# Attention and a routed expert layer on one core: the product of a head pair moved behind the next pair's first two scores, the sums of v kept in its tile, the gate arithmetic moved to GpSimd

## The chip, the cores and the metric

The kernel runs on one core of one Trainium2 chip. The metric is the device time of one execution in microseconds: 448.46 us, the median of two runs (448.41 and 448.5). The profile is of one further execution with a span of 449.2 us. A slot below is a unit of the written order, not of time.

## What is computed

Two layers follow one another. The first is attention over 8 batches and 12 heads, 448 positions of 64, with a softmax whose denominator has an extra 1:

```python
scores = scale * np.matmul(q, k.transpose(0, 1, 3, 2))
m = np.max(scores, axis=-1, keepdims=True)
e = np.exp(scores - m)
attn = e / (np.sum(e, axis=-1, keepdims=True) + np.exp(-m) + 1e-09)
return np.matmul(attn, v)
```

Multiplied through by exp(m), the weights are exp(s) / (sum of exp(s) + 1). The second layer takes the 3584 rows of 768 numbers, finds the nearest of 8 expert vectors by cosine and applies that expert:

```python
logits = xn @ en.T / tau
expert_idx = np.argmax(logits, axis=1)
gate_w = probs[np.arange(N), expert_idx]     # softmax of the logits, at the chosen expert
h = np.maximum(x[mask] @ w1[e], 0.0)         # 768 x 1024
out[mask] = gate_w[mask, None] * (h @ w2[e]) # 1024 x 768
```

## The kernel before

**Tiling.** Work on attention goes by head pairs: 12 heads make 6 pairs in a batch (`NP`), 48 pairs in all. A pair's queries and keys are transposed by TensorE with an identity (`front_qk`, L193 and L194), so that each of the two heads holds 64 partitions, and copied to SBUF: keys by ScalarE (L203), queries by VectorE (L208). The scores come with the key position in the partitions. Tiles 0, 1 and 2 hold 128 key positions of both heads (L235); tile 3 holds the last 64 positions of the two heads, one head in each half of the partitions (L241). ScalarE takes the exponential (L246, L248), VectorE subtracts one (L254, L257). What is multiplied with v is exp(s) - 1, and the sum over v itself is added afterwards: hence "sums of v".

**The product** (`attend`, L270 and L275) has one accumulation for each head. Its weights are `vab`: 64 columns of v and 64 columns of ones, so that 64 output rows hold the product and 64 the sum of exp(s) - 1. In the kernel before, both heads have the order v, ones; the product is always in rows 0 to 63. ScalarE turns the sums into 1/(1 + sum/449) by Ln (L285) and Exp of the negative (L289), VectorE adds the sum of v and multiplies (`normalise`, L303), and a bf16 copy for the experts follows (`low`, L312). A square of x for the norm follows (`square`: GpSimd for the first pairs, ScalarE from pair 11 on).

**Sums of v.** GpSimd adds the four pieces of v (`sum_v`, L180 to L182). A matmul with a column of ones adds over the partitions (L198), two pairs at a time, into two free columns of the tile of the transposes. VectorE copies them to SBUF as `sv` (L213), where `normalise` reads them as scalars.

**Router.** When a batch's six pairs are done, `router_mm` multiplies with the expert vectors and with ones (L335, 24 matmuls), the result is copied (L341) and transposed (`router_tok`, L349). VectorE finds the chosen expert of each token (`router_logits`), a matmul counts them (`router_pick`, L414), VectorE finds the most frequent expert (`router_count`), and GpSimd loads its index and fetches its weights by seven DMAs (`fetch`, L447). The gate is worked out by `router_pow` (a square root as a power on GpSimd, L375), `router_exp` (VectorE, L381 to L383), `router_act` (ScalarE, L389) and `router_gate` (VectorE, L395 to L408). Tokens of other experts have a path of their own at the end.

**Experts.** A batch has 15 chunks: eight of h (6 matmuls each, L487) and seven of y (8 or 16 matmuls, L515, L534). A chunk fills one PSUM tile `work`, which VectorE or ScalarE then empties (L495, L497, L505, L507). The chunks of a batch are strewn over six later pairs, twelve pairs behind its attention (`LAG`).

**Order.** The order on every engine is written out by hand. `put(slot, fn)` files a piece under a number; the pieces are emitted in rising order of it, and each engine runs its own in that order. Pair g has the numbers from 8g (`NSLOT` = 8). A piece's number says where it stands in the queues, and not when it runs. Chunks stand at the offsets `FILL`: three in an even slot and two in an odd one. `late` has, for each offset, the number at which the chunk's tile is emptied, and whether VectorE does it. Before, the product of pair g stands at 3.35 of the slot after its own, ahead of score tile 3 of the next pair (its neighbours are score tile 2 at 3.3 and tile 3 at 3.4).

**Buffers in PSUM.** `work` has 2 tiles of one bank (chunks, score tile 3, warm-up, the router's transposes), `big` 2 tiles of two banks (transposes, score tiles 0 to 2, the router product), `av` one tile of two banks (the product). A new tile waits until the last but one of its kind is emptied, for `av` the last one.

Of the kernel before, what the change touches and what calls it, by code (L numbers as in the profile page):

```python
# [28 lines left out]
FILL = ((0.8, 3.2, 5.6), (0.8, 5.6))  # L29
# [7 lines left out]
def build_consts(k):  # L37
# [26 lines left out]
    for s in range(2):  # L64
        va = pool.tile([128, 4, 4, 64], F32R, name=f"vab{s}")
        for h in range(2):
            nc.vector.tensor_copy(
                out=va[:, :, 2 * h + 1, :],
                in_=k.ones_f[:, 0:1].unsqueeze(2).broadcast_to([128, 4, 64]),
            )  # L70
        k.vab.append(va)


def build_late_consts(k):
# [11 lines left out]
    nc.vector.memset(k.half[:], 0.5)  # L86
    k.rr = pool.tile([128, 512], F32, name="rr")
# [98 lines left out]
def front_qk(k, g, s):  # L186
# [8 lines left out]
    if i == GP - 1:  # L195
        vs = k.va.pop(n)
        for j in range(GP):
            nc.tensor.matmul(ps[:, 0, S + j : S + j + 1], lhsT=vs[:, 2 * j : 2 * j + 2, :], rhs=k.ones_f[:],  # L198
                             start=True, stop=True)

# [5 lines left out]
    def q_out():  # L206
        qt = k.qt.tile([128, S], F32R, name="qt", tag="qt")
        nc.vector.tensor_copy(out=qt[:], in_=ps[:, 0, 0:S])  # L208
        k.qts[g] = qt
        if i == GP - 1:  # L210
            k.sv[n] = k.svp.tile([64, GP, 2], F32, name="sv", tag="sv")
            for h in range(2):
                nc.vector.tensor_copy(out=k.sv[n][:, :, h], in_=ps[64 * h : 64 * h + 64, 0, S : S + GP])  # L213

    k.put(s + 0.6, k_out)
    k.put(s + 0.7, q_out)


# [44 lines left out]
def attend(k, g, s, b=None):  # L263
# [4 lines left out]
    for h in range(2):  # L268
        r = slice(64 * h, 64 * h + 64)
        nc.tensor.matmul(  # L270
            ps[:, h, 0:S], lhsT=va[r, 3, 2 * h : 2 * h + 2, :], rhs=k.ems[g, 3][r, :], start=True, stop=False,
        )
    for j in range(3):
        for h in range(2):
            nc.tensor.matmul(  # L275
                ps[:, h, 0:S], lhsT=va[:, j, 2 * h : 2 * h + 2, :], rhs=k.ems[g, j][:, h, :],
# [3 lines left out]
    if b is not None:  # L280
        router_pick(k, b, ps[:, 0, S : S + 4 * E])

    def log():
        k.rd[g] = k.rdp.tile([128, 2, S], F32, name="rd", tag="rd")
        nc.scalar.activation(k.rd[g][64:128], ps[64:128, :, 0:S], ACT.Ln, bias=1.0, scale=1.0 / (S + 1.0))  # L285

    def recip():
        rd = k.rd.pop(g)
        nc.scalar.activation(rd[64:128], rd[64:128], ACT.Exp, scale=-1.0)  # L289
        k.avs[g] = ps, rd  # L290

    k.put(s + 1.45, log)
    k.put(s + 1.65, recip)


def normalise(k, g, s):
# [4 lines left out]
    sv = k.sv[g // GP]  # L301
    for h in range(2):
        nc.vector.scalar_tensor_tensor(  # L303
            out=x[64 * h : 64 * h + 64, :], in0=ps[0:64, h, 0:S], scalar=sv[:, g % GP, h : h + 1],
            in1=rd[64:128, h, :], op0=ALU.add, op1=ALU.mult,
# [8 lines left out]
    k.put(s + 1.6, low)  # L314
# [12 lines left out]
def router_mm(k, b, s):  # L327
# [13 lines left out]
    k.put(s + 1.75, lambda: nc.scalar.copy(out=k.rr[:, 0:S], in_=ps[:, 0:S]))  # L341


def router_tok(k, b, s):

    nc, p = k.nc, k.rp
    tp = k.work.tile([128, 4, 128], F32, name="work", tag="work")
    for t in range(4):
        nc.tensor.transpose(tp[:, t, :], k.rr[:, 128 * t : 128 * t + 128], k.ident[:])  # L349
    k.put(s + 0.8, lambda: router_logits(k, b, tp))  # L350
# [27 lines left out]
def router_exp(k, b):  # L378
    nc, p = k.nc, k.rp
    l, nrm = k.lg[b]  # L380
    nc.vector.tensor_scalar_add(nrm[:], nrm[:], 1e-6 * (S + 1.0))  # L381
    nc.vector.reciprocal(out=nrm[:], in_=nrm[:])
    nc.vector.tensor_tensor(out=l[:], in0=l[:], in1=nrm[:].unsqueeze(2).broadcast_to([128, 4, E]), op=ALU.mult)  # L383
# [8 lines left out]
def router_gate(k, b):  # L392
    nc, p = k.nc, k.rp
    gate = p.tile([128, 4], F32, name="gate", tag="gate")
    nc.vector.reduce_sum(out=gate[:], in_=k.lg.pop(b)[:], axis=AX.X)  # L395
    nc.vector.tensor_scalar_add(gate[:], gate[:], 1e-9)
    nc.vector.reciprocal(out=gate[:], in_=gate[:])
# [386 lines left out]
```

The softmax here doesn't subtract the row's maximum and nothing guards it: scores larger than these inputs give would overflow.

## Time and profile before

| what | us |
|---|---|
| time, median of two runs | 448.46 |
| span of the profiled execution | 449.2 |
| product of pair 0, 11, 46, 47 begins | 22.05, 103.36, 390.32, 396.78 |
| one exponential of 128x896 (L246, mean) | 0.915 |
| one subtraction of 128x896 (L254, mean; median) | 0.731; 0.622 |
| one half of normalise (L303, mean) | 0.677 |
| one power on GpSimd (L375, mean) | 1.160 |

A name such as L246 is a line of the kernel. PE is TensorE, PEld its loading of weights, DVE VectorE, ACT ScalarE, POOL GpSimd and SP the engine that issues most DMAs. In lists of waits a line says who waited, for whom, the sum in us, how often, and the longest. In the chain of waits a line has the start, the length and the work; it is followed back from the end of the execution, at each step to what released it. Busy time of PE is not PE at its peak, since its matmuls overlap and their ends are modelled.

### The profile page before, as it was taken

To read this page: it belongs to the slowest core of one execution; us is meant where nothing else is said; L and a number is where in the kernel's file an instruction comes from. 1 tells how busy PE (TensorE), PEld (TensorE's weight loads), DVE (VectorE), ACT (ScalarE), POOL (GpSimd) and SP (SyncE) were. 2 spreads that over 40 slices of the span, in tenths; PEclk is the share of its full clock that TensorE was granted. 3 is DMA by queue.
4 is the path that set the end of the run, shared out by engine and by line. 5 is a ranking of instruction groups with operands and counts; after the bars stand their busy time and mean duration, and the time that the engine had idled before them with its cause. 6 is when DMAs were issued, how large, how long until landed. Compare 5 with 4: busy or idle time off the path is not lost.

```text
span 449.2 us, 7412 instructions
## 1 busy us (share of the span) xinstructions
PE 402.3 (90%) x2430; PEld 239.4 (53%) x2430; DVE 338.4 (75%) x771; ACT 318.9 (71%) x440; POOL 135.6 (30%) x170
## 2 busy tenths in 40 slices
PE   7977789778989999899989999899989998999696
PEld 3545454545556556555565555665666556545243
DVE  2569987998699769996799769986999769754222
ACT  1578877787797888788787878788879878751111
POOL 4115442745156004700074003800372006105100
PEclk9699999999999999999999999999999999999889
DMA  8775345799479966997589857998499507913963
GB/s 175 174 175 127 72 101 124 138 167 222 101 145 202 208 165 128 203 199 204 123 167 212 218 122 147 205 187 212 95 188 219 151 1 135 216 54 51 238 118 126
DMA packets 133690, 69.77 MB, mean 155 GB/s; under 512 B 99848, under 2 KB 127496, under 8 KB 133648
## 3 DMA queue, kind: packets, MB, share of 16 engines
q1 hardware_dynamic: 115392, 43.63, 39.1%
q0 software_dynamic: 16384, 25.17, 33.4%
q10 hardware_dynamic: 1872, 0.46, 0.5%
q8 instruction: 20, 0.33, 0.3%
q14 instruction: 22, 0.18, 0.1%
HBM read 83.39 MB, written 16.52 MB: 222 GB/s over the span
## 4 chain that ended last, share of the span: by engine, by line
PE 62%; DVE 24%; DMA 5%; ACT 5%; issue 3%; SPq 1%; POOL 0%; POOLq 0%; ACTq 0%; DVEq 0%
PE work L487 15%; PE av L275 10%; PE work L515 7%; PE big L235 6%; PE big L193 6%; DVE em L254 6%; PE rmm L335 4%; DVE x L303 4%; PE work L631 4%; DVE y L505 3%; DMA w<-in_moe_w_dram 2%; DVE xb L312 2%; PE work L534 2%; ACT e L246 2%; DVE h L495 2%
## 5 line engine op out<-in xcount | busy, mean ns | idle before, releaser
L246 ACT ACTIVATE e<-big 128x896 f32<-128x896 f32 x144 | 126.6, 915 | 24.3 <-PE big L235 23.7
L254 DVE TENSOR_SCALAR em<-e 128x896 fp32r<-128x896 f32 x144 | 102.7, 731 | 17.4 <-ACT e L246 17.3
L487 PE MATMUL work<-xb,w 128*128 128x448 bf16 x384 | 84.1, 360 | 12.3 <-DVE h L495 7.2
L515 PE MATMUL work<-w,h 128*128 128x384 bf16 x384 | 69.3, 326 | 4.3 <-DVE y L505 4.3
L303 DVE SCALAR_TENSOR_TENSOR x<-av,sv,rd 64x448 f32<-64x448 f32 x96 | 65.0, 677 | 8.7 <-ACT rd L289 6.7
L275 PE MATMUL av<-em,vab 128*128 128x448 f32 x288 | 70.9, 381 | 0.0
L487 PEld LDWEIGHTS <-w 128*128 128x128 bf16 x384 | 36.9, 102 | 52.3 <-issue 23.3
L285 ACT ACTIVATE rd<-av 64x896 f32<-64x896 f32 x48 | 43.8, 912 | 25.7 <-PE av L275 19.9
L375 POOL TENSOR_TENSOR nrm<-nrm,half 128x4 f32<-128x4 f32 x8 | 9.3, 1160 | 171.3 <-DVE nrm L357 171.3
L235 PE MATMUL big<-qt,kt 64*128 64x448 f32 x288 | 55.7, 436 | 5.0 <-DVE qt L208 4.5
L275 PEld LDWEIGHTS av<-em,vab 128*128 128x128 f32 x288 | 50.3, 188 | 16.6 <-issue 13.9
L495 DVE TENSOR_SCALAR h<-work 128x448 bf16<-128x448 f32 x40 | 24.9, 623 | 42.3 <-PE work L487 40.5
L447 POOL DMA_DIRECT2D w<-in_moe_w_dram x56 | 42.9, 776 | 39.1 <-DVE h L495 15.6
L515 PEld LDWEIGHTS <-h 128*128 128x128 bf16 x384 | 35.5, 99 | 33.0 <-issue 13.0
L203 ACT CAST kt<-big 128x512 fp32r<-128x512 f32 x48 | 28.1, 585 | 28.1 <-PE big L198 15.8
L289 ACT ACTIVATE rd<-rd 64x896 f32<-64x896 f32 x48 | 45.5, 947 | 1.5
L235 PEld LDWEIGHTS big<-qt,kt 64*128 64x128 f32 x288 | 23.8, 186 | 38.3 <-issue 20.5
L208 DVE CAST qt<-big 128x448 fp32r<-128x448 f32 x48 | 29.5, 615 | 10.0 <-ACT kt L203 9.6
L193 PE MATMUL big<-ident,qm 128*128 128x128 f32 x144 | 25.1, 284 | 11.5 <-ACT e L246 11.5
L505 DVE TENSOR_SCALAR y<-work,g 128x384 f32<-128x384 f32 x32 | 19.7, 615 | 17.5 <-PE work L515 14.8
L631 PE MATMUL work<-ident 128*128 128x512 bf16 x96 | 30.3, 421 | 2.8 <-POOL ident masks.py:199 1.7
L507 ACT ACTIVATE y<-work,g 128x384 f32<-128x384 f32 x24 | 13.9, 580 | 22.7 <-PE work L515 15.7
(102 smaller groups left out, 546.1 us busy)
## 6 DMA issues: line engine op xcount, KB each, us to landing
w<-in_moe_w_dram POOLq DMA_DIRECT2D x24, 512.0 KB, 6.2
w<-in_moe_w_dram POOLq DMA_DIRECT2D x32, 384.0 KB, 10.0
qm<-in_q_dram SPq DMA_DIRECT2D x72, 128.0 KB, 3.1
vld<-in_v_dram SPq DMA_DIRECT2D x24, 384.0 KB, 3.6
out_dram<-y SPq DMA_DIRECT2D x48, 192.0 KB, 2.9
km<-in_k_dram SPq DMA_DIRECT2D x69, 128.0 KB, 3.2
qrest<-in_q_dram SPq DMA_DIRECT2D x24, 64.0 KB, 2.9
vld<-in_v_dram SPq DMA_DIRECT2D x48, 32.0 KB, 3.2
```

Source lines behind the costliest of these rows:

```text
L193: nc.tensor.transpose(ps[:, m, 128 * j : 128 * j + 128], x[:, j, 2 * i : 2 * i + 2, :], k.ident[:])
L235: nc.tensor.matmul(ps[:, h, 0:S], lhsT=kt[64 * h : 64 * h + 64, 128 * j : 128 * j + 128], rhs=qt[64 * h : 64 * h + 64, :], start=True, sto ...
L246: nc.scalar.activation(e[:], ps[:, :, 0:S], ACT.Exp, scale=scale)
L254: nc.vector.tensor_scalar_sub(em[:], e[:], 1.0)
L275: nc.tensor.matmul(ps[:, h, 0:S], lhsT=va[:, j, 2 * h : 2 * h + 2, :], rhs=k.ems[g, j][:, h, :], start=False, stop=(j == 2),)
L285: nc.scalar.activation(k.rd[g][64:128], ps[64:128, :, 0:S], ACT.Ln, bias=1.0, scale=1.0 / (S + 1.0))
L289: nc.scalar.activation(rd[64:128], rd[64:128], ACT.Exp, scale=-1.0)
L303: nc.vector.scalar_tensor_tensor(out=x[64 * h : 64 * h + 64, :], in0=ps[0:64, h, 0:S], scalar=sv[:, g % GP, h : h + 1], in1=rd[64:128, h, ...
L447: k.nc.gpsimd.dma_start(w[:], src)
L487: nc.tensor.matmul(ps[:, 0:S], lhsT=w1[c // 2][:, c % 2, 128 * f : 128 * f + 128], rhs=xb[:, c, :], start=(c == 0), stop=(c == NP - 1),)
L515: nc.tensor.matmul(ps[:, 0:SM], lhsT=hs[f][:, 128 * t : 128 * t + 128], rhs=w2[f // 2][:, f % 2, SM * n : SM * n + SM], start=(f == 0), st ...
L631: nc.tensor.matmul(ps[:], lhsT=idb[:, 0:128], rhs=idb.unsqueeze(1).broadcast_to([128, 2, 256]), start=True, stop=True)
```

## The change

The product of pair g moves to 0.1 of the next slot, right behind score tiles 0 and 1 of pair g+1. The scores are thus what TensorE does while the last operand of the product is prepared. All other offsets are set anew around this.

The second head's weights become ones, v, so that its product lies in rows 64 to 127 and its sums in rows 0 to 63. Both heads share one block of ones in `vab`. One matmul per pair now puts the sums of v of both heads into column 448 of the product's own tile, where `normalise` reads them as scalars in the partitions where they are needed. The copies `sv` go. Ln and Exp run over all 128 partitions in one go, product rows included; the rows that are not sums are not used.

The gate's arithmetic goes to GpSimd: reciprocals become powers of -1 (`less`), and the chosen expert's part (`own`) is summed apart and multiplied by the gate afterwards. Two sums stay on VectorE. The router's steps stand some three to eight numbers earlier, most of them; its transposes use `big` instead of `work`, and the pick stands in its own place behind the product of the following slot.

```diff
-FILL = ((0.8, 3.2, 5.6), (0.8, 5.6))
+FILL = ((2.8, 5.3, 5.4), (2.8, 5.4))
...
-        va = pool.tile([128, 4, 4, 64], F32R, name=f"vab{s}")
+        va = pool.tile([128, 4, 3, 64], F32R, name=f"vab{s}")
...
-            nc.tensor.matmul(ps[:, 0, S + j : S + j + 1], lhsT=vs[:, 2 * j : 2 * j + 2, :], rhs=k.ones_f[:],
-                             start=True, stop=True)
...
-            k.sv[n] = k.svp.tile([64, GP, 2], F32, name="sv", tag="sv")
-            for h in range(2):
-                nc.vector.tensor_copy(out=k.sv[n][:, :, h], in_=ps[64 * h : 64 * h + 64, 0, S : S + GP])
-
-    k.put(s + 0.6, k_out)
-    k.put(s + 0.7, q_out)
+    k.put(s + 1.1, k_out)
+    k.put(s + 2.1, q_out)
...
-                ps[:, h, 0:S], lhsT=va[:, j, 2 * h : 2 * h + 2, :], rhs=k.ems[g, j][:, h, :],
+                ps[:, h, 0:S], lhsT=va[:, j, h : h + 2, :], rhs=k.ems[g, j][:, h, :],
...
+    i = g % GP
+    nc.tensor.matmul(ps[:, 0, S : S + 1], lhsT=k.va[g // GP][:, 2 * i : 2 * i + 2, :], rhs=k.ones_f[:], start=True, stop=True)
...
-        nc.scalar.activation(k.rd[g][64:128], ps[64:128, :, 0:S], ACT.Ln, bias=1.0, scale=1.0 / (S + 1.0))
...
-        nc.scalar.activation(rd[64:128], rd[64:128], ACT.Exp, scale=-1.0)
...
-    k.put(s + 1.45, log)
-    k.put(s + 1.65, recip)
+        nc.scalar.activation(rd[:], ps[:, :, 0:S], ACT.Ln, bias=1.0, scale=1.0 / (S + 1.0))
+        nc.scalar.activation(rd[:], rd[:], ACT.Exp, scale=-1.0)
+
+    k.put(s + 2.3, recip)
...
+        r, o = slice(64 * h, 64 * h + 64), slice(64 - 64 * h, 128 - 64 * h)
         nc.vector.scalar_tensor_tensor(
-            out=x[64 * h : 64 * h + 64, :], in0=ps[0:64, h, 0:S], scalar=sv[:, g % GP, h : h + 1],
-            in1=rd[64:128, h, :], op0=ALU.add, op1=ALU.mult,
+            out=x[r, :], in0=ps[r, h, 0:S], scalar=ps[r, 0, S : S + 1], in1=rd[o, h, :], op0=ALU.add, op1=ALU.mult,
...
-    tp = k.work.tile([128, 4, 128], F32, name="work", tag="work")
+    tp = k.big.tile([128, 4, 128], F32, name="tok", tag="big")
...
-    nc.vector.tensor_scalar_add(nrm[:], nrm[:], 1e-6 * (S + 1.0))
-    nc.vector.reciprocal(out=nrm[:], in_=nrm[:])
-    nc.vector.tensor_tensor(out=l[:], in0=l[:], in1=nrm[:].unsqueeze(2).broadcast_to([128, 4, E]), op=ALU.mult)
+    nc.gpsimd.tensor_scalar_add(nrm[:], nrm[:], 1e-6 * (S + 1.0))
+    nc.gpsimd.tensor_tensor(out=nrm[:], in0=nrm[:], in1=k.less[:], op=ALU.pow)
+    nc.gpsimd.tensor_tensor(out=l[:], in0=l[:], in1=nrm[:].unsqueeze(2).broadcast_to([128, 4, E]), op=ALU.mult)
...
+        nc.vector.reduce_sum(out=gate[:], in_=k.lg.pop(b)[:], axis=AX.X)
+        nc.vector.reduce_sum(out=own[:], in_=gm[:], axis=AX.X)
...
+        nc.gpsimd.tensor_scalar_add(gate[:], gate[:], 1e-9)
+        nc.gpsimd.tensor_tensor(out=gate[:], in0=gate[:], in1=k.less[:], op=ALU.pow)
...
+        nc.gpsimd.tensor_tensor(out=g0[:], in0=own[:], in1=gate[:], op=ALU.mult)
...
-        put(s - NSLOT + 4, lambda n=n: sum_v(k, n))
+        put(s + 1.2, lambda n=n: sum_v(k, n))
...
-        put(s - NSLOT + 2.3, lambda g=g, s=s - NSLOT + 2.3: front_qk(k, g, s))
-        put(s + 5.9, lambda g=g: front_v(k, g))
-        for j, o, pa, pv in ((0, 0, 0.3, 1.5), (1, 0.05, 0.4, 2.5), (2, 3.3, 3.6, 4.6), (3, 3.4, 5.1, 8.2)):
+        put(s - NSLOT + 4.2, lambda g=g, s=s - NSLOT + 4.2: front_qk(k, g, s))
+        put(s + 0.8, lambda g=g: front_v(k, g))
+        for j, o, pa, pv in ((0, 0, 0.3, 1.5), (1, 0.05, 0.4, 2.6), (2, 5.2, 6, 7.7), (3, 0.15, 2.6, 7)):
...
-        put(s + 3.35, lambda g=g, s=s, b=pick: attend(k, g, s + 3.35, b))
-        put(s + 7, lambda g=g, s=s: normalise(k, g, s + 7))
-        put(s + NSLOT + 3.1, lambda g=g: square(k, g))
+        put(s + 0.1, lambda g=g, s=s: attend(k, g, s + 0.1))
+        put(s + 4.75, lambda g=g, s=s: normalise(k, g, s + 4.75))
+        put(s + 7.1, lambda g=g: square(k, g))
...
-        for o in (0.8, 3.2, 5.6):
-            put(g * NSLOT + o, lambda: warm(k, 2))
+        for o in (2.8, 5.4):
+            put(g * NSLOT + o, lambda: warm(k, 3))
...
+        put(s + 2.75, lambda b=b, s=s: router_mm(k, b, s + 2.75))
+        put(s + 7.9, lambda b=b, s=s: router_tok(k, b, s + 7.9))
         s += NSLOT
...
+        put(s + 0.16, lambda b=b: router_pick(k, b))
+        put(s + 0.9, lambda b=b: router_pow(k, b))
+        put(s + 3.5, lambda b=b: router_count(k, b))
+        put(s + 4.3, lambda b=b: router_index(k, b))
+        for i, o in enumerate((4.4, 10, 16, 25, 31, 37, 43)):
...
+        put(s + 4.5, lambda b=b: router_exp(k, b))
+        put(s + 7.2, lambda b=b: router_act(k, b))
         s += NSLOT
...
+        put(s + 3.5, lambda b=b: keep_rows(k, b))
+        put(s + 5.5, lambda b=b: keep_xb(k, b))
+        put(s + 6, lambda b=b, s=s: router_gate(k, b, s + 6))
+
+    late = {2.8: (4.7, False), 5.3: (7.3, True), 5.4: (8.5, True)}
```

## The prediction

> **What bounds the kernel now.** I read the head of the page first, for the engines' shares.
>
> ```profile
> span 449.2 us, 7412 instructions
> PE 402.3 (90%) x2430; PEld 239.4 (53%) x2430; DVE 338.4 (75%) x771; ACT 318.9 (71%) x440; POOL 135.6 (30%) x170
> ```
>
> PE is nearly full, so the question is what its missing tenth consists of, and in which stage. The starts of the product (L270) cut the span: pair 0 at 22.05 us, pair 11 at 103.36, pair 46 at 390.32, pair 47 at 396.78. That is 22.1 us of lead-in, 11 distances of 7.39 us without expert work, 36 of 8.15 us with it (293.4 us), and 52.4 us of tail. The table by stretches gives the busy time in the last three, then in six pairs of full operation:
>
> ```profile
> 22.00:103.40 81.40, 65.99 (x390) 38.77 (x388) 70.12 (x138) 63.04 (x82) 34.30 (x36) 1.00 0.61 132
> 103.40:397.00 293.60, 274.88 (x1724) 169.33 (x1720) 242.28 (x558) 238.69 (x332) 86.95 (x106) 1.00 0.80 168
> 397.00:449.20 52.20, 42.66 (x249) 21.95 (x247) 16.94 (x50) 9.28 (x16) 7.19 (x9) 0.93 0.52 115
> 219.70:269.30 49.60, 46.35 (x293) 28.65 (x292) 41.62 (x94) 40.24 (x56) 14.37 (x18) 1.00 0.83 176
> ```
>
> Columns after the length: PE, its weight loads, DVE, ACT, POOL, clock, DMA. In the middle PE is the bound, with DVE and ACT over 80% full. Early on DVE is fuller than PE, so there a chain over several engines sets the pace. PE's waits, for the lead stage and then the middle:
>
> ```profile
> PE big L193 <- ACT e L246: 11.2, 9, 1.6
> ...
> PE work L487 <- DVE h L495: 6.3, 12, 1.3
> PE work L534 <- DVE y L505: 5.3, 6, 0.9
> PE work L515 <- DVE y L505: 3.9, 6, 0.8
> ```
>
> Early, the next pair's transposes wait for an exp to empty a `big` tile; later, chunks wait until DVE has emptied a `work` tile. The chain of waits over a pair with two chunks shows both the prices and such a wait:
>
> ```profile
> 202.59 0.21 PE av L270 x2
> 202.80 1.42 PE av L275 x6
> 204.22 0.02 issue
> 204.24 0.64 DVE h L495
> 204.88 0.04 issue
> 204.92 1.30 PE work L487 x6
> 206.22 0.60 PE big L235 x4
> 206.82 1.24 PE work L487 x6
> 208.06 0.33 PE big L193 x3
> ```
>
> From this chain PE's prices are: two score tiles back to back 0.60 us, one alone 0.40, the 64-row score 0.20, product 1.61, transposes of a pair 0.88, sums of v 0.34 for two pairs, an h chunk 1.24, a y chunk 1.33, the router product 2.39, its transposes 0.59. A pair without chunks costs 0.88 + 1.00 + 0.20 + 1.61 + 0.17 = 3.86. Six pairs: 6 x 3.86 + 8 x 1.24 + 7 x 1.33 + 2.98 = 45.4 us. Measured from product to product they take 49.4, 49.6 and 48.9. Only about 4 us in six pairs can be won in the middle.
>
> **What the Trainium skill says.** "SBUF — State Buffer", Who interferes with whom: GpSimd shares a port pair with DVE, and a tensor_scalar or cast in a two-port mode is blocked for a whole GpSimd instruction. The trace agrees: L254 takes 607 ns at least and 1167 at most, and the long ones lie beside POOL work. "GPSIMD Engine Reference", Engine selection: two-input elementwise work is about twice as slow there as on DVE. The trace has an intercept too: 128x256 takes about 0.73 us undisturbed and 128x448 1.11, so 2.0 ns an element and 0.22 us fixed; I estimate 0.23 to 0.3 us for the small gate operations, and take the power's 1.16 us from L375. "TensorE: Matmul & The Clock Gate", What's actually happening: about 3.4 us of idleness halves PE's clock. In the tail, after a 3.1 us wait for weights, h matmuls are 0.37 us apart instead of 0.21.
>
> **The change, part by part.** PE loses and gains nothing: the same product, the same number of sum matmuls and warm-up matmuls. Only waits can go.
>
> *Deleted DVE work:* 48 copies of sums x 0.151 = 7.2 us (L213). Moved to GpSimd: L381 to L383 (0.289 + 0.178 + 0.244) and the add, reciprocal, products and copy of the gate (0.227 + 0.178 + 0.426 + 0.264 + 0.147), eight times: 15.6 us. That is 22.8 of 338 us, 2.8 us in six pairs. It relieves the stretch from 222 to 244 us, where the chain ran through DVE for nearly three pairs. Ln and Exp now take 128 partitions instead of 64 at the same 896 elements a partition: I cost it at nothing, as L246 takes 915 ns on 128 partitions and L285 takes 912 on 64. Reading the scalar from PSUM has no row; between 0 and 0.15 us (a whole small copy, as L213) for each of 96 operations, and I take 0, because it is one value a partition beside 448 that already come from PSUM.
>
> *The new order.* The product of pair g now stands behind two score tiles of g+1. Let it start at 0. Ln waits for product and sum: 1.61 + 0.17 + 0.05 = 1.83. Ln 0.92 and Exp 0.95 end at 3.72 with dispatch. ACT then takes in order exp of the 64-row score (0.54), the first chunk's release (0.56), the copy of k (0.59) and the third exp (0.92), to 6.33; DVE's subtraction (0.62) makes the last operand of the next product ready at 7.0. This loop through ACT is a floor of 7.0 us per pair. DVE's own loop is normalise 3.74 to 5.11, copy of q to 5.7, short subtraction to 6.1, a second chunk's release to 6.7, last subtraction to 7.3, inside PE's time where that chunk exists. PE's own sum is 3.86 + 2 x 1.28 = 6.42 in odd slots and 7.70 in even ones. So odd slots take 7.0 (PE waits 0.6), even ones 7.7: three of each are 44.1.
>
> *Chunks and buffers.* With two `work` tiles, each allocation needs the last but one emptied. In the new order that is always an ACT or DVE release due earlier in the same or previous slot: the long tile of DVE waits above goes, apart from the 0.6.
>
> *Router slot.* PE gets 2.98 more, of which 0.6 fills the odd slot's wait: +2.4. In the next slot DVE has six logits operations (1.2 us) and the count (1.0) ahead of normalise, which then begins at about 4.0 instead of 3.74; 0.3 is hidden below PE's 7.7. New wait: the router's exp on ACT stands behind GpSimd's queue of register load (1.6 us from the index, as at 223 us), DMA issue 0.76, add 0.25, power 1.16, product 0.28. By this sum it ends at about 7.7 to 8.0 and ACT's next score exp, due at 7.6, queues behind it: 0.4 us, of which the following slot swallows most. I charge 0.4 per batch in all. Six pairs: 44.1 + 2.4 + 0.4 = 46.9, and 36 pairs 281.4, against 293.4.
>
> *First twelve pairs.* Without chunk release and square on ACT the loop is 6.4 us. The square on GpSimd (1.12) starts right after normalise, beside the two subtractions that the product needs: between 0 and 0.9 more. I take 6.9: 11 x 6.9 + 1.3 for the router = 77.2, against 81.3.
>
> *Lead-in.* First scores stay at 11.5. The product came at +3.35 of slot 1 and now comes at +0.1: two exps to 13.7, the short one to 14.3, the half-clock transposes to 15.5, copy of k and third exp to 17.2, subtraction 17.9. Product 0 at 18.0, against 22.05.
>
> *Tail.* From product 47: PE has 1.8 + 30 chunks (37.5) + router 3.0 = 42.3. Two of those chunks came earlier before. The pick now follows the router's transposes with nothing between: PE waits for the logits, 1.4 us. Weights of the last batch: first fetch about 14.9 after the product (before: 13.8), and the third piece's issue must wait behind the power and the row scatter, about 5 us after the first instead of 2.8. PE reaches that batch at about 25.2. The third piece landed 11.1 us after its issue before, so at 28 to 31: 3 to 6 us idle (before 3.1), then about 3 us of half clock. With 1 for releases and 4.4 from the last matmul to the end: 42.3 + 1.4 + 4.5 + 3 + 1 + 4.4 = 56.6.
>
> Sum: 18.0 + 77.2 + 281.4 + 56.6 = 433.2 on the profile's scale, 0.7 less on that of the times: 432.5, taken as 433.
>
> **The rivals.** *ACT's loop becomes the full bound* (chance 0.20): if anything in it is longer by 0.5 us (each link 0.05 more for its semaphore, or the two normalise operations slower by their PSUM scalar), odd slots take 7.5 and even ones 7.9, six pairs 49.0, and the early pairs 7.3: 18 + 81.6 + 294 + 57 = 450, less 0.7: no change. For it: L246 already shows ACT waiting 23.7 us for scores. Against: ACT has only 40.2 us of work in six pairs.
>
> *GpSimd takes it back* (0.13): gate arithmetic and sums blocking a subtraction in each pair (+0.5, as L254's worst) and the router's exp held up by more than 2 us in each batch: 8.6 per pair in the middle, 7.7 early: 18 + 86 + 310 + 57 = 471, slower. For it: DVE's g_all (L398) took 426 ns in place of 190 beside POOL. Against: the sums run while DVE waits between its second subtraction and normalise.
>
> *PE truly becomes the bound* (0.12): ACT gets ahead in odd slots too, as in the long router slot; 45.4 for six pairs, 6.45 early, no longer stall in the tail: 17.8 + 72.3 + 272.4 + 54 = 416.
>
> **How the numbers follow.** The forecast has 0.55 and spreads from 424 to 441. Leaving out most of the slower case and the lower edge of the last, the range is 419 to 452. Faster by over 2% (below 439.5): nearly all of 0.55, all of 0.12: 0.66. Within 2%: 0.20. Slower: 0.14.
>
> **What would show it.** Distances of the product of 7.0 and 7.7 by turns and about 9.4 at the router; the waits of L487, L515 and L534 for DVE nearly gone, and in their place a wait of the product's first matmul for the last subtraction. Product 0 near 18. In the tail a wait of the pick for the logits, and again weights. I am wrong if the product's wait is above 1 us per pair, if ACT waits for GpSimd at the router by more than 1 us, or if subtractions of 1.1 us become the rule.

## The result, and the profile after

The changed kernel takes 431.46 us (431.28 to 431.64) against 448.46: the ratio is 0.962, with a 95% interval of 0.958 to 0.966. The forecast was 433.0 within 419 to 452. The total came out as forecast; of the reasons behind it, some did not. By the starts of the product (now L257) the spans divide so:

| stage | before | forecast | after |
|---|---|---|---|
| up to product 0 | 22.05 | 18.0 | 17.09 |
| products 0 to 11 | 81.31 | 77.2 | 80.53 |
| products 11 to 47 | 293.42 | 281.4 | 280.53 |
| product 47 to the end | 52.4 | 56.6 | 51.95 |

The early stage is 3.3 us longer than forecast and the tail 4.7 us shorter. These two misses nearly cancel. A third error helped as well. On the profile's scale the forecast was 433.2 and the span is 430.1, and the prediction took 0.7 us off to come to the times. But the profiled execution of the kernel before took 450.71 us for its span of 449.2, and that of the changed kernel 431.64 for 430.1, so 1.5 us have to be added. That the total lies within 1.5 us of the forecast is in part luck.

The head of the page of the changed kernel:

```profile
span 430.1 us, 7384 instructions
PE 400.0 (93%) x2430; PEld 248.1 (58%) x2430; DVE 314.8 (73%) x658; ACT 305.3 (71%) x440; POOL 171.7 (40%) x242
```

VectorE lost 23.6 us of work and GpSimd gained 36.1: a power there costs a microsecond where a reciprocal on VectorE cost 0.18. The table by stretches, of the last three stages and of six pairs of full operation (the same columns as before: PE, its weight loads, DVE, ACT, POOL, clock, DMA):

```profile
17.10:97.60 80.50, 67.89 (x378) 43.21 (x375) 65.64 (x121) 60.13 (x81) 35.60 (x44) 0.96 0.66 143
97.60:378.10 280.50, 276.12 (x1736) 175.63 (x1734) 225.97 (x473) 229.68 (x335) 120.15 (x164) 1.00 0.81 172
378.10:430.10 52.00, 42.69 (x263) 22.83 (x263) 17.34 (x45) 10.07 (x18) 11.06 (x18) 1.00 0.61 133
255.43:302.26 46.83, 46.20 (x293) 29.47 (x292) 37.62 (x80) 38.39 (x57) 19.85 (x28) 1.00 0.85 186
```

In the middle PE is busy for 276.1 of 280.5 us. Six pairs take 46.83 us, of which PE is busy for 46.20. The kernel before had 46.21 us of PE work in such six pairs and took 48.87 us (269.35 to 318.22 us): the work of PE is the same and most of its idle time has gone. Its waits between products 11 and 47 (who waited, for whom: us, times, longest):

```profile
PE big L222 <- DVE qt L200: 1.2, 6, 0.2
PE work L513 <- issue: 1.2, 4, 0.3
PE work L513 <- ACT e L235: 0.7, 2, 0.4
```

The 15.5 us in which chunks waited for VectorE to empty `work` are no longer there. The chain of waits over a slot with two y chunks consists of PE alone:

```profile
184.52 0.60 PE big L222 x4
185.12 0.20 PE av L257 x2
185.32 1.42 PE av L262 x6
186.74 0.12 PE av L268 x2
186.85 0.31 PE work L228
187.16 1.32 PE work L513 x8
188.48 0.33 PE big L191 x3
```

The product (L257, L262) follows two score tiles without a gap, then come the sum of v (L268), score tile 3 (L228) and a chunk. The distances of the product over six pairs, from the router's slot on, are 9.54, 7.68, 7.26, 8.27, 6.63 and 7.46 us.

### The profile page after: what moved, and what is told of

It reads as the page before. It is cut to its first block, busy times and chain, and to the rows that moved or that the text cites. A ratio compares the mean times of both kernels' runs of the same rounds, so it can differ in the third digit from the quotient of the medians.

```text
span 430.1 us, 7384 instructions
## 1 busy us (share of the span) xinstructions
PE 400.0 (93%) x2430; PEld 248.1 (58%) x2430; DVE 314.8 (73%) x658; ACT 305.3 (71%) x440; POOL 171.7 (40%) x242
## 4 chain that ended last, share of the span: by engine, by line
PE 56%; DVE 20%; ACT 11%; issue 5%; POOL 4%; DMA 3%; POOLq 1%; DVEq 0%; ACTq 0%
PE av L262 11%; PE work L513 10%; PE work L485 8%; PE big L222 7%; DVE x L286 5%; PE big L191 4%; PE rmm L317 4%; DVE em L241 4%; DVE qt L200 4%; ACT e L233 3%; ACT rd L274 3%; DMA w<-in_moe_w_dram 3%; ACT rd L273 3%; PE work L629 2%; PE work L532 2%
## 5 line engine op out<-in xcount | busy, mean ns | idle before, releaser
L233 ACT ACTIVATE e<-big 128x896 f32<-128x896 f32 x144 | 127.6, 921 | 32.1 <-PE big L222 31.4
L241 DVE TENSOR_SCALAR em<-e 128x896 fp32r<-128x896 f32 x144 | 96.9, 687 | 7.2 <-ACT e L233 6.8
L286 DVE SCALAR_TENSOR_TENSOR x<-av,rd 64x448 f32<-64x448 f32 x96 | 66.3, 691 | 46.7 <-ACT rd L274 36.4
L485 PE MATMUL work<-xb,w 128*128 128x448 bf16 x384 | 79.7, 353 | 1.3 <-DMA w<-in_moe_w_dram 0.8
L262 PE MATMUL av<-em,vab 128*128 128x448 f32 x288 | 73.1, 391 | 0.0
L222 PE MATMUL big<-qt,kt 64*128 64x448 f32 x288 | 56.8, 435 | 15.8 <-DVE qt L200 15.0
L262 PEld LDWEIGHTS av<-em,vab 128*128 128x128 f32 x288 | 51.5, 192 | 16.2 <-issue 13.1
L485 PEld LDWEIGHTS <-w 128*128 128x128 bf16 x384 | 34.9, 98 | 39.4 <-issue 9.8
L273 ACT ACTIVATE rd<-av 128x896 f32<-128x896 f32 x48 | 44.1, 919 | 17.4 <-PE av L268 11.2
L445 POOL DMA_DIRECT2D w<-in_moe_w_dram x56 | 45.2, 809 | 27.0 <-issue 23.0
L222 PEld LDWEIGHTS big<-qt,kt 64*128 64x128 f32 x288 | 24.3, 184 | 43.1 <-ACT e L233 14.4
L200 DVE CAST qt<-big 128x448 fp32r<-128x448 f32 x48 | 29.9, 624 | 24.1 <-ACT kt L195 22.8
L274 ACT ACTIVATE rd<-rd 128x896 f32<-128x896 f32 x48 | 45.7, 952 | 1.5
L503 DVE TENSOR_SCALAR y<-work,g 128x384 f32<-128x384 f32 x32 | 19.6, 614 | 15.4 <-PE work L513 11.2
L209 DVE CAST vab<-vld 128x512 fp32r<-128x512 f32 x48 | 29.4, 612 | 0.0
L303 POOL TENSOR_TENSOR xs<-x 128x448 f32<-128x448 f32 x11 | 10.3, 933 | 40.5 <-DVE x L286 34.7
```

Of the source, the lines that this page charges most:

```text
L222: nc.tensor.matmul(ps[:, h, 0:S], lhsT=kt[64 * h : 64 * h + 64, 128 * j : 128 * j + 128], rhs=qt[64 * h : 64 * h + 64, :], start=True, sto ...
L233: nc.scalar.activation(e[:], ps[:, :, 0:S], ACT.Exp, scale=scale)
L241: nc.vector.tensor_scalar_sub(em[:], e[:], 1.0)
L262: nc.tensor.matmul(ps[:, h, 0:S], lhsT=va[:, j, h : h + 2, :], rhs=k.ems[g, j][:, h, :], start=False, stop=(j == 2),)
L273: nc.scalar.activation(rd[:], ps[:, :, 0:S], ACT.Ln, bias=1.0, scale=1.0 / (S + 1.0))
L274: nc.scalar.activation(rd[:], rd[:], ACT.Exp, scale=-1.0)
```

## Experiments

Two theories can explain the middle stage. A, that of the prediction: the new order took the waits away. B: relieving VectorE (the copies of the sums gone, the gate arithmetic moved) would have done it without the new order, since before it was VectorE that emptied `work` late. Three runs put parts of the change into the old order, three take parts out of the new one.

### The gate arithmetic alone, in the kernel before

`router_exp` and `router_gate` are those of the changed kernel; all places in the order stay.

```diff
-    nc.vector.reciprocal(out=nrm[:], in_=nrm[:])
+    nc.gpsimd.tensor_tensor(out=nrm[:], in0=nrm[:], in1=k.less[:], op=ALU.pow)
```

> The kernel before with the gate arithmetic on GpSimd alone, everything else in the old order. Theory B (freed VectorE work brings the time): its share, 15.6 of the 22.8 us freed, of the 17 us won: 435 to 440 us. Theory A (the order brings it): 444 to 449 us.

Measured: 444.60 us, ratio 0.991 (0.988 to 0.994). This is in the range of A.

### The sums of v alone, in the kernel before

The layout of `vab` with one block of ones, the sums in the product's tile, Ln and Exp on 128 partitions; the gate and all places stay.

```diff
-lhsT=va[:, j, 2 * h : 2 * h + 2, :]
+lhsT=va[:, j, h : h + 2, :]
...
-scalar=sv[:, g % GP, h : h + 1]
+scalar=ps[r, 0, S : S + 1]
```

> The kernel before with the new layout alone: sums of v in the product's tile and read there, ones shared, Ln and Exp over 128 partitions; order and gate arithmetic as before. Theory B: its share of the freed VectorE time, 7.2 of 22.8 us, of the 17 us won: 441 to 444 us. Theory A: 445 to 449 us. In both, if reading the scalar from PSUM costs VectorE nothing, a half of normalise takes 0.67 to 0.69 us as before; if it costs a small copy's time, 0.75 or more.

Measured: 443.88 us, ratio 0.987 (0.981 to 0.994). This is in the range of B. Each part gains about one per cent by itself, and apart from each other they do not decide between A and B. What PE still waited for (100 to 375 us), with the gate moved:

```profile
PE work L500 <- DVE h L508: 7.8, 12, 1.0
PE work L528 <- DVE y L518: 2.5, 5, 0.5
```

and with the sums moved:

```profile
PE work L522 <- DVE y L493: 5.3, 6, 0.9
...
PE work L475 <- DVE h L483: 1.1, 6, 0.2
```

The two edits shorten different waits. In the same stretch the kernel before waits 6.3 us for h and 7.9 for y. With the sums moved it is mainly the waits for h that go (1.1 now), with the gate moved mainly those for y (2.5 now).

### Both parts in the old order

The two edits above together: all that the change does, except the places in the order.

> The kernel before with both other parts of the change, the new layout and the gate arithmetic on GpSimd, and the old order: what it lacks of the changed kernel is the order alone. The two parts alone measured 0.9874 and 0.9907 of before, 5.7 and 4.2 us. If their gains add and the order brings the rest of the 17 us: 438 to 441 us, six pairs in the middle about 47.5 us against 46.8 with the new order. If the order alone is worth little: under 434. If the two gains come from the same waits and don't add: 442 to 444.

Measured: 434.88 us, ratio 0.972 (0.967 to 0.977). The table by stretches, between products 0 and 11, 11 and 47, and over the six pairs:

```profile
18.93:98.27 79.34, 66.12 (x386) 39.77 (x384) 65.61 (x120) 61.50 (x82) 38.70 (x45) 1.00 0.66 144
98.27:380.58 282.31, 275.11 (x1727) 174.57 (x1724) 224.41 (x474) 230.43 (x332) 120.69 (x162) 1.00 0.83 169
257.95:305.02 47.07, 46.26 (x293) 29.50 (x291) 37.47 (x81) 38.83 (x56) 20.18 (x28) 1.00 0.91 191
```

and its PE waits in the middle:

```profile
PE work L488 <- DVE h L496: 2.2, 5, 1.6
PE work L516 <- DVE y L506: 1.0, 6, 0.2
```

The time lies in none of the expected ranges: the two parts together win 2.8 per cent, where their single gains add up to 2.2. Of the 12.9 us that the middle stage won, 11.1 come without any new order, and six pairs take 47.07 us against 46.83. The new order adds 1.8 us in the middle and 1.8 us in the lead-in, and costs 1.2 us early: 434.88 against 431.46 us in all, under one per cent, with intervals that just do not meet. So the relief alone is enough for most of the gain in the middle. Whether the order alone would be enough too is the question of the next runs.

### The parts taken out of the new order

Gate arithmetic back on VectorE, with its reciprocals:

```diff
-    nc.gpsimd.tensor_tensor(out=nrm[:], in0=nrm[:], in1=k.less[:], op=ALU.pow)
+    nc.vector.reciprocal(out=nrm[:], in_=nrm[:])
```

> The changed kernel with the gate arithmetic back on VectorE (reciprocals instead of powers), at the same places in the order. Theory A (the new order of the product brings the time, and the gate arithmetic on GpSimd is worth little, because ScalarE then waits 1.6 to 3.4 us per batch for it): 428 to 435 us, ScalarE's wait for GpSimd gone, VectorE 15 us busier. Theory B (freeing VectorE brings the time): two thirds of the freed VectorE time come back, so 440 us or more.

Measured: 434.22 us, ratio 0.966 (0.960 to 0.972). Next, the sums copied from the product's tile to SBUF again and read there:

```diff
+        nc.vector.tensor_copy(out=sv[64 * h : 64 * h + 64, :], in_=ps[64 * h : 64 * h + 64, 0, S : S + 1])
...
-scalar=ps[r, 0, S : S + 1]
+scalar=sv[r, :]
```

> The changed kernel with the sums of v copied from the product's tile to SBUF by VectorE, two small copies of 64x1 in each pair ahead of normalise, which reads them there. If reading the scalar from PSUM costs something, a half of normalise goes from 0.691 us back to 0.677. The copies wait only for the product, not for Exp, so they fall into VectorE's wait ahead of normalise: 430 to 433 us. If VectorE's work were the bound in the new order, 96 copies of about 0.15 us would bring 434 us or more.

Measured: 433.45 us, ratio 0.966 (0.961 to 0.970). Both intervals overlap that of the changed kernel. By the medians each part is worth two to three microseconds in the new order (the second run puts back the copies alone, not the rest of the layout). The middle stage tells it more sharply: 283.5 us with the gate on VectorE and 282.1 with the copies, against 280.5, while three runs below that leave this stage alone have 280.5 to 281.0. In the old order each part was worth four to six by itself, and by the ratios seven to eight beside the other. This fits that the order and the relief remove the same waits, so that what one has removed the other can't win again. It is against A, which gave the order the credit, and also against B as a statement about the changed kernel. If the 3.0 and 1.6 us of the middle stage simply added, the order alone would keep about 8 of the 12.9 us: an estimate, since no run has the new order without both parts.

The last run also prices the scalar read from PSUM, in the groups of the page; first with copies, then in the changed kernel:

```profile
L289 DVE SCALAR_TENSOR_TENSOR x<-av,sv,rd 64x448 f32<-64x448 f32 x96 | 65.6, 683 | 24.0 <-ACT rd L274 21.3 <-DVE sv L286 0.7
```

```profile
L286 DVE SCALAR_TENSOR_TENSOR x<-av,rd 64x448 f32<-64x448 f32 x96 | 66.3, 691 | 46.7 <-ACT rd L274 36.4 <-PE big L191 7.7 <-PE rmm L317 1.6
```

The mean is 691 ns with the scalar in PSUM and 683 with it in SBUF: 8 ns an operation, which justifies the nothing that I had put down.

### The product back in the slot's middle

```diff
-        put(s + 0.1, lambda g=g, s=s: attend(k, g, s + 0.1))
+        put(s + 2.85, lambda g=g, s=s: attend(k, g, s + 2.85))
...
-    k.put(s + 2.3, recip)
+    k.put(s + 0.02, recip)
```

The pick moves to 2.86 with it.

> The changed kernel with the product behind the slot's first chunk instead of right behind the first two scores (Ln and Exp then behind the exp of the short score tile); all else stays. Theory A (the chain scores, product, Ln, Exp, normalise, copy of q, next scores sets the distance wherever TensorE does not): the chunk's 1.25 us enter the chain, 7.3 us per pair early and 7.9 in the middle: 442 to 452 us, TensorE waiting for the copy of q. Theory B (freed VectorE work and sums in the tile bring the time, the product's place does not matter): 429 to 435.

Measured: 525.26 us, ratio 1.169 (1.161 to 1.177). Its waits over the whole execution:

```profile
DVE x L286 <- ACT rd L274: 153.2, 40, 7.3
ACT rd L273 <- PE av L268: 99.2, 37, 5.6
```

In ScalarE's queue Ln (L273) moved back only behind the exponential of the short score tile. So it waits up to 5.6 us for a product that comes later, and the chunk's release, the copy of k and the third exponential, which still stand behind it, wait as well. The early distances grow to between 7.8 and 12.5 us, and the middle ones to 8.7 to 12.3. The direction was foreseen and the size was not, by any theory. The run shows that the new offsets hang together. It does not measure the new place by itself: the kernel with both parts in the old order, whose other offsets suit the old place, is the fairer comparison.

### Is there a loop through ScalarE of 7.0 us?

The prediction's floor of 7.0 us ends in the subtraction for the product's last operand. If the product really had to wait for that operand, it would lose nothing by reading it sooner; if there is a slack, it would lose that slack. Score tile 2 is read first of the three:

```diff
-    for j in range(3):
+    for j in (2, 0, 1):
```

> The changed kernel with the product's matmuls in another order: the operand that is ready last (score tile 2) right behind the short one, instead of at the end. Theory: the floor of 7.0 us per pair that the prediction put on the loop through the last subtraction does not show, because that operand is wanted only about 1.2 us after the product begins. Then taking this slack away brings a wait of TensorE for the last subtraction of 0.2 to 1.0 us in most slots: 440 to 450 us. Rival: the last operand is ready before the product begins anyway, as TensorE is behind: under 433 us, no such wait.

Measured: 440.35 us, ratio 0.979 (0.972 to 0.986). Its waits of PE over the whole execution:

```profile
PE big L222 <- DVE qt L200: 10.8, 10, 2.1
PE av L262 <- DVE em L241: 9.8, 17, 0.6
```

Here the wait of the product for the subtraction (L241) appears: 9.8 us in 17 places, where the changed kernel has none. So in these places the changed order profits from reading that operand last, 1.2 us after the product's start (from the chain above: 0.20 for the product's two matmuls with score tile 3 and four of the six matmuls of 1.42 make 1.15).

The places matter. Twelve of the 17 waits, 6.8 us, are at the second and third product behind a router slot, where the last subtraction ends 0.8 and 1.0 us after the product's start in both kernels. In the short slots nothing changes: they take 6.63 us in both. There the last subtraction ends 6.75 us after the start of the product before, 0.12 after the start of its own, and even this run reads it only at 0.30. So 7.0 us is no floor, for two reasons: in these slots the operand is ready 0.25 us sooner than the prediction's sum said, and the product needn't wait for it to start.

The time grows by 8.9 us, but not all of that is the price of these waits. The middle stage grows by 4.7 us and the early one by 5.2, of which nearly 3 lie in one slot (9.54 instead of 6.70), around which the granted clock is 0.66 (24 to 34 us).

### GpSimd's queue at the router

The changed kernel's longest wait of ScalarE for GpSimd reads `ACT l L371 <- POOL l L365` with 15.5 us in eight waits, up to 3.4. In the first router slot it lies on the chain of waits:

```profile
72.97 0.67 issue
73.65 0.95 POOL w L445
...
74.67 0.70 POOL nrm L363
...
75.46 1.08 POOL nrm L364
...
76.62 0.25 POOL l L365
...
77.03 1.71 ACT e L233 x2
```

The power and the product with the norm (L364, L365) stand behind the loading of the expert's index and the issue of its first weights (L445), though they need neither. Two exponentials of scores (L233), which need nothing of the router, stand behind them on ScalarE. In the next run the arithmetic is put ahead of the index:

```diff
-        put(s + 4.5, lambda b=b: router_exp(k, b))
+        put(s + 1.3, lambda b=b: router_exp(k, b))
```

> The changed kernel with the scaling of the logits (add, power, product on GpSimd) ahead of the register load and the first weight fetch instead of behind them. If ScalarE's wait for GpSimd at the router's exp delays the normalise, the copy of q and so the next scores (it is up to 3.4 us early on, and two slots around the router take 0.2 and 0.6 us more than TensorE's work in them): 425 to 428 us, with the wait of ScalarE for GpSimd under 2 us in all. If that wait is hidden under TensorE's work: 430.5 to 432.5.

Measured: 428.24 us, ratio 0.955 (0.949 to 0.962), at the upper edge of the first range. The wait is gone from the list; the second slot behind each router slot falls from 7.26 to 6.78 us, and in the first batch from 8.22 to 7.69. Six pairs:

```profile
253.30:299.70 46.40, 46.27 (x294) 29.40 (x292) 37.99 (x80) 38.49 (x57) 19.74 (x28) 1.00 0.87 188
```

PE is now busy for 46.27 of 46.40 us. The middle stage takes 277.7 us instead of 280.5. The intervals of this kernel and the changed one overlap, but the place and the size of the gain in the traces agree with the cause.

### The first twelve pairs

Here the forecast was 3.3 us too low. It blamed GpSimd's square for part of each distance. With the square on ScalarE throughout:

```diff
-    if g < LAG - 1:
+    if False:
```

> The changed kernel with the first eleven squares on ScalarE too, so that no square on GpSimd lies beside a subtraction early on. If the loop through normalise and the copy of q sets the early distance (6.65 us), it stays between 6.6 and 6.8: 430 to 432 us. If the blocked subtractions set it, as the prediction had it with 0.5 us, early distances fall to 6.2: 425 to 427 us.

Measured: 429.95 us, ratio 0.958 (0.954 to 0.962); the early stage takes 79.70 us instead of 80.53. The first two distances are 6.56 and 6.60 instead of 6.62 and 6.70. So moving the squares wins 0.1 us a pair, of the 0.5 that I had charged for them. The run does not test blocked subtractions in general. In the trace of the changed kernel none of the eleven squares overlaps a subtraction of a large tile. All 20 long ones (0.96 us and more, of 144) lie beside GpSimd's additions of v (L178 to L180). Nor do these set the distance: pair 1 has a last subtraction of 1.15 us and comes 6.62 us after pair 0, pair 2 has one of 0.61 and comes 6.70 after pair 1. What sets the distance is in the chain of the changed kernel:

```profile
24.19 1.42 PE av L262 x6
25.61 0.13 PE av L268 x2
...
25.76 0.93 ACT rd L273
...
26.71 0.96 ACT rd L274
...
27.70 0.68 DVE x L286
...
28.39 0.70 DVE x L286
...
29.13 0.63 DVE qt L200
29.76 0.14 issue
29.89 0.49 PE big L222 x2
```

It is a loop: product, Ln, Exp, both halves of normalise, the copy of the queries (L200), and the next scores that need it. PE's waits name it: the scores L222 wait for L200 for 11.7 of the 80.5 us. To break this loop the next pair's transposes and copies were put ahead of normalise for these pairs:

```diff
-        put(s - NSLOT + 4.2, lambda g=g, s=s - NSLOT + 4.2: front_qk(k, g, s))
+        fo = 0.06 if 0 < g < LAG else 4.2
+        put(s - NSLOT + fo, lambda g=g, s=s - NSLOT, fo=fo: front_qk(k, g, s, fo))
```

The copies of k and q stand at 0.45 and 1.4 then.

> The changed kernel with, in the first twelve pairs only, the next pair's transposes right behind the first two scores, and the copies of k and q ahead of Ln and of the first subtractions. Theory: without chunks the distance of 6.65 us is the loop scores, product, Ln, Exp, normalise, copy of q, scores, since the copy of q stands behind normalise. Taken out of it, early pairs come every 5.7 to 6.1 us: 421 to 426 us, and TensorE's wait for the copy of q early on falls from 11 us to under 3. Rival: the GpSimd squares beside the subtractions set the distance: above 429 us.

Measured: 439.73 us, ratio 0.979 (0.972 to 0.986). Of the 8.3 us lost, 3.9 lie ahead of product 0, which starts at 21.0 us after a granted clock of 0.50 (12 to 18 us), and 5.2 in the early stage; 0.9 come back in the tail. The early distances are mostly 7.07 us, one slot behind the first router takes 11.9, and PE now waits 8.2 us for an exponential to empty a `big` tile. This fits another, longer loop in the place of the first. The time is in the rival's range, but the run does not speak for the rival, since the squares stayed where they were. That the loop through normalise is the bound follows from the chain, and was not shown by removing it.

One early slot takes 7.65 us, and its granted clock is low (0.76 between 38 and 45 us). Longer warm-up matmuls, on top of the earlier arithmetic, were to raise it:

```diff
-            put(g * NSLOT + o, lambda: warm(k, 3))
+            put(g * NSLOT + o, lambda: warm(k, 5))
```

> The faster version so far (logits scaled ahead of the register load) with five warm-up matmuls in place of three at each place in the first twelve pairs. In the profiles so far PE's clock stood at 0.76 in the mean between 38 and 45 us, and the distance there was 7.65 instead of 6.65. If too little work in the slots before is the cause, the distance becomes 6.7 and the time 1 us less than 0.9554 of before: 0.951 to 0.955. If the extra matmuls lengthen early slots instead: above 0.957.

Measured: 427.21 us, ratio 0.953 (0.950 to 0.956). In the table by stretches, the changed kernel and then this one, over the same seven microseconds:

```profile
38.00:45.00 7.00, 6.46 (x29) 4.34 (x29) 6.78 (x14) 4.89 (x7) 2.70 (x4) 0.76 0.36 94
```

```profile
38.00:45.00 7.00, 5.77 (x34) 3.42 (x33) 6.82 (x15) 4.75 (x7) 1.94 (x3) 1.00 0.55 135
```

and the run of the next section, which has three warm-up matmuls and the changed kernel's instructions up to its last batch:

```profile
38.00:45.00 7.00, 4.91 (x30) 3.03 (x29) 6.82 (x15) 4.70 (x8) 1.85 (x3) 1.00 0.62 153
```

The clock is full with the longer warm-up, and the slot takes 7.62 us all the same. The clock is also full in the third line, where the slot takes 7.61. So this stretch does not show what the warm-up did for the clock, and the clock is not what sets this slot: VectorE is busy for 6.8 of the 7 us in all three, which fits as its limit. The early stage as a whole is not shorter than with the earlier arithmetic alone (80.05 against 79.95 us). What the longer warm-up seems to change is the spread: all five executions have a mean granted clock of at least 0.999 and lie within 0.7 us, where the four with the earlier arithmetic alone have 0.984 to 0.996 and lie within 3.9. The difference of their medians, 1.0 us, is less than the intervals tell apart. This is the fastest version measured, and its interval lies wholly below that of the changed kernel.

### The weights of the last batch

Would earlier issues shorten the waits for weights in the tail? The four fetches of the second matrix follow the first three at once:

```diff
-        for i, o in enumerate((4.4, 10, 16, 25, 31, 37, 43)):
+        for i, o in enumerate((4.4, 10, 16, 25, 31, 37, 43) if b < B - 1 else (4.4, 10, 16, 16.1, 16.2, 16.3, 16.4)):
```

> The changed kernel with the last batch's four w2 fetches issued right behind its third w1 fetch, ahead of the gate arithmetic. Theory: the tail came out better than predicted because the w2 fetches, held back by the gate's power on GpSimd, left the third w1 piece the bandwidth, 7.5 us from issue to use instead of 11. Then the first h chunk of the last batch waits 2 to 4 us for weights here, perhaps with PE's clock at half after it, the y chunks' wait of 2.0 us goes, and the time is 431 to 436 us. Rival: the third piece lands at the same time whatever else is under way: 429 to 430 us, by the 2.0 us of the y chunks.

Measured: 431.84 us, ratio 0.962 (0.955 to 0.969): the changed kernel's time. The wait of y for its weights is 1.90 us instead of 1.97, that of h 0.56 instead of 0.75. The time is in the range of the theory, but the waits that it expected did not come, nor did the rival's gain. When these later pieces are issued does not matter here. The changed kernel's timeline in the tail shows why (start, length, instruction):

```profile
392.78 0.73 POOL L445 DMA_DIRECT2D w<-in_moe_w_dram  x1 [2.38 <-DVE tot L587]
...
398.06 0.81 POOL L445 DMA_DIRECT2D w<-in_moe_w_dram  x1
...
404.15 0.92 PE L485 MATMUL work<-xb,w 128*128 128x448 bf16 x4
405.83 8.51 PE L485 MATMUL work<-xb,w 128*128 128x448 bf16 x44 [0.75 <-DMA w<-in_moe_w_dram]
417.28 1.78 PE L513 MATMUL work<-w,h 128*128 128x384 bf16 x10 [1.97 <-DMA w<-in_moe_w_dram]
```

The long run of h matmuls starts 13.1 us after the first issue in this kernel, 12.8 with the early fetches, and 14.0 before (410.55 to 424.59). But from the third issue it is 7.8 us here, where the prediction had counted 11.1. Counted from the first issue, the third piece of the last batch landed after 14.0, 13.0 and 12.8 us in these three kernels; counted from its own issue, after 11.2, 7.7 and 7.5. This fits three pieces of 512 KB that behave as one stream, timed from its beginning. It is no constant: in the changed kernel's other batches, whose third issue comes 7 to 9 us after the first, it took 13.0 to 16.2 us from the first.

## Why the prediction was right, and where it was not

**The middle, 281.4 forecast and 280.5 measured: right in size, wrong in its cause.** The step "The new order" gave the gain to the order, and mentioned the deleted work on VectorE only as relief of one stretch. The runs show that the relief by itself, in the old order, brings 11.1 of the 12.9 us; what the order would bring by itself stays open. What hid this from me was my own list of waits: all three large ones named VectorE as the late engine, and that calls for less work on VectorE before it calls for a new order. That PE would be the limit after either is what made the size right.

**The floor of 7.0 us did not show.** The failed step is "makes the last operand of the next product ready at 7.0": it let the product start when its last operand is ready, whereas that operand is read about 1.2 us after the start. The run that reads it first made the missing wait appear behind the routers and early. The sum itself was too long as well: in the short slots, which take 6.63 us, the operand is ready at 6.75. Beside it, other slots were longer than the 7.7 forecast (8.27), and the sum over six pairs came out at 46.83 against 46.9 by these errors cancelling.

**The router on ScalarE: the cost about right, the wait too short.** Forecast 0.4 us per batch; taking the wait away gave 0.5 per batch in the middle (7.26 to 6.78) and 0.5 in the first batch (8.22 to 7.69), about 3 us in the time. ScalarE waits 1.9 us on average (15.5 by 8), so my own mark for being wrong, more than 1 us, was passed. That the following slot swallows most of it is why the cost stayed small.

**The early stage, 77.2 forecast and 80.5 measured.** Two terms failed. The base of 6.9 was made of a loop of 6.4 and 0.5 for the square; the trace has mostly 6.62 to 6.71, by its chain the loop through normalise and the copy of the queries. The square wins 0.1 when it is moved and lies beside no subtraction. The term "+ 1.3 for the router" is the large miss: the four distances around the first router are 9.09, 7.53, 8.22 and 7.56, together 5.8 us more than four of 6.65. Without chunks PE has no work there behind which the router could hide: the chain goes from its transposes through VectorE's logits and count to GpSimd's queue and ScalarE. Only the last piece of this, 0.5 us, was shown by a run.

**The lead-in, 18.0 forecast and 17.1 measured.** The order's part is smaller than the 5.0 us that the stage lost. The kernel with only the gate moved, which keeps the old order, starts its first product at 19.02, and the one with both parts at 18.93. The granted clock (the last figure but two) from 14 to 18 us is half in the profile of before and full in that of the kernel with only the gate moved:

```profile
14.00:18.00 4.00, 4.00 (x15) 2.21 (x14) 2.05 (x10) 1.50 (x3) 1.47 (x3) 0.50 0.88 220
```

```profile
14.00:18.00 4.00, 3.73 (x22) 1.82 (x22) 3.15 (x14) 3.56 (x5) 1.40 (x2) 1.00 0.87 209
```

So about 3 us of the 5 go with the clock of that one profile, whose execution took 450.71 us instead of the median 448.46, and 1.8 are left for the order. That figure is rough: the run with the earlier second matrix, whose instructions are the changed kernel's up to the last batch, starts its first product at 16.20 instead of 17.09. The Trainium skill, "TensorE: Matmul & The Clock Gate", section "What's actually happening", says that the window in which the clock is judged runs freely, so that the cold start differs from run to run of one kernel. The runs agree in that the clock differs: nine executions of the kernel before had a mean granted clock from 0.983 to 0.996 and took 450.15 to 445.92 us. Where in an execution the difference lies is shown by the profiles alone.

**The tail, 56.6 forecast and 52.0 measured.** The wait of the pick for the logits came at 1.3 us (forecast 1.4), the last batch's first fetch at 14.6 after the product (14.9), its third issue 5.3 after the first (5). The failed term is "3 to 6 us idle, then about 3 us of half clock". It timed the third piece from its own issue instead of the stream from its start: the piece landed 27.6 us after the product, against 28 to 31. And PE had work until 26.9 us, against the 25.2 from which the wait was counted; this is nearly half of the difference. PE waited 0.75 us, and the clock stayed at 1.00. The waits for weights and the lost clock were put at 7.5 us and came to 2.7 (0.75 and 1.97): this step is the miss.

**Of the rivals,** none came true as a whole. ScalarE's loop as the full bound is refuted by the slots of 6.63. Of the case that GpSimd takes it back, a small part is true: subtractions of 1.07 us next to GpSimd's work do occur around the first router (2.15 for two in that chain), in agreement with what the prediction took from the Trainium skill, "SBUF — State Buffer", Who interferes with whom. But they lie beside the additions of v (L179, L180) and not beside the gate's arithmetic, and the mean of L241, against L254 before, fell from 731 to 687 ns. PE as the true bound is what the middle is, at its measured busy time of 46.2 us in six pairs and not at the 45.4 of summed prices.

What stays open: the new order without the relief of VectorE was not run, so that what the order would win by itself is not known. Beside the relief it wins 3.4 us.

## What to carry to other kernels

When PE waits for an engine to empty a tile, also try to take work off that engine and see what is left before rearranging the order; the two can win the same microseconds. In a loop over several engines, count to the moment at which an operand is read, not to the start of the operation that reads it, and read the operand that comes last at the end. A small operation of another engine is as late as all that stands ahead of it in its queue: put it ahead of loads and issues that it does not need.

## What I had not expected of the hardware

Three transfers of 512 KB that are issued one after another over 5.3 us ended as one: 13.0 us after the first issue and 7.7 after the third, and 12.8 after the first when later fetches were issued sooner. The same opening came to its first product at 16.20 us in one execution and at 17.09 in another. Waits of PE of 0.8 and 2.0 us in the tail left the granted clock at 1.00, where the kernel before, after 3.1 us, had shown 0.93 over that stage. And a scalar operand read from PSUM cost 8 ns in an operation of 691.
